# Attention weights turned unnormalized, with the reciprocal sums applied to the logits and the token rows

## The chip, the core and the metric

The kernel runs on one core of a Trainium2 chip. The metric is the time of one execution in device microseconds (us). The core has a matrix engine (PE, with its weight loads shown apart as PEld), a vector engine (DVE), a scalar engine (ACT) and a general engine (POOL), each working through its own instructions in order; a queue processor (SP) and POOL also issue transfers to and from memory.

## What is computed

Causal attention over a window of 128 positions, with a linear bias, for 8 batches of 576 tokens and 8 heads of 64, and behind it a mixture of 8 experts. A token picks its expert afresh or keeps that of the token before it, by the sign of a gate. Both the choice and the gate use linear maps of the attention's output.

```
scores = q @ k.T / 8 - slope[h] * |i - j|      where 0 <= i - j < 128, else -1e9
attn   = exp(scores - max);  attn = attn / (sum(attn) + 1e-9)
x      = (attn @ v), heads side by side        # [8, 576, 512]
logits = x @ w_gate;  local = sigmoid(x @ w_local)
e      = argmax(logits) if s == 0 or local < 0.5 else e of token s - 1
out    = softmax(logits)[e] * (relu(x @ w1[e]) @ w2[e])
```

The division by the sum is a factor per token and head. It can be applied to the weights, or later to the 64 columns of x that belong to the head.

## The kernel before, in words

**Attention.** The work is cut into 32 slots, one for a pair of heads of one batch (4 slots a batch), and a slot into 9 blocks of 64 queries. The function `spread` reads the list `ORDER[p]`, a table written out by hand, and emits one piece of work for each of its letters; since each engine works in program order, this table sets the order on all of them. A letter without a mark is work of the slot itself, one mark (`'`) means the slot before, two marks the one before that. Per slot the pieces are:

- `S` products of q and k on PE into tiles `sc` (four PSUM buffers); `D` bias, mask and row maximum on DVE (`scs`, `mn`); `E` the exponential on ACT, which also writes the row sums `sm`; its result lies in one of two buffers `PB`, shown in the trace as the tile `cut`.
- `R` adds 1e-9 to the sums and takes the reciprocal `r` on DVE, in three groups; `N` multiplies each of the 9 blocks of weights by its reciprocals on POOL, in place.
- `U` turns weights on PE (tile `pt`), `C` copies them out (`pts`, on DVE for `C0`, else on ACT), `M` multiplies them with v on PE (`xa`), `X` copies the result to `xT` on ACT, `T` transposes it on DVE into a buffer `T`. After the last `T` of a batch SP writes this buffer to memory (`xd`), as rows of tokens.

A dot in the table advances a side program by one step: `tokens(b)` (logits from `xT`, on PE, ACT and DVE) and `route(b)` (the expert of each token, its place in a table, and five scatters of entries to the table `t4` on POOL, the rows `t<-pay,to`). It begins with `X1` of the last pair of a batch, two slots late. Colons advance `setup`, which makes constants on POOL and also blanks `t4` in memory. In the last two batches POOL also gathers token rows of the first experts (`kr<-xd`, `wraw<-xd`), and ACT and DVE split the first weights.

**Experts.** Each weight chunk is cut into a high and a low part (ACT and DVE), and PE does three products for each pair of parts (lines 878 to 880, tiles `h` and `y`). The first two experts get only tokens of the first batches, so they can start before the last batch is routed; the third needs all of it: `tokens(7)` and `route(7)` then run as a side program of the first two (`routing`), one step with each `tick`, then come the table, the gathers on POOL and the turning of the rows on DVE.

Of the kernel before, what the change touches and what calls it, by code (L numbers as in the profile page):

```python
# [8 lines left out]
F32 = mybir.dt.float32  # L9
# [7 lines left out]
P = 128  # L17
# [33 lines left out]
def windows(nb):  # L51
# [6 lines left out]
ORDER = [  # L58
# [4 lines left out]
]  # L63
# [8 lines left out]
def moe_attention(ctx, tc, qT, kT_d, vv, wg, wl, w1, w2, out):  # L72
# [24 lines left out]
    msel = cp.tile([P, 4], F32, name="msel")  # L97
    roff = cp.tile([P, 1], F32, name="roff")
    first = cp.tile([P, NT], F32, name="first")
    w32 = cp.tile([P, 4, 32], F32, name="w32")  # L100
# [224 lines left out]
    with ExitStack() as actx:  # L325
# [11 lines left out]
        for s in range(3):  # L337
            V.append([ap.tile([P, n, P], F32, name=f"v{n}{z}{s}") for n, z in ((4, 0), (4, 1), (5, 2))])
        for s in range(2):
# [39 lines left out]

        loaded = load(0)  # L380

        warm = ap.tile([P, P], F16, name="warm")
        T = [ap.tile([P, SB, 4, 32], F32, name=f"T{s}") for s in range(2)]
        dve.memset(warm, 0.0)
        pw = ptk.tile([P, 512], F32, name="pk")
# [13 lines left out]
        for h in range(2):  # L399
            for z in range(2):  # L400
                dve.memset(slope[halves[h], z:z + 1], -4.0 if h == z else -2.0)
        for p in range(4):
            make_bias(p)
# [6 lines left out]
        def setup():  # L410

            whole = dict(channel_multiplier=0, allow_small_or_imprecise_dtypes=True)
            pool.memset(w32, 0.0)
            nc.sync.dma_start(w32[:, :, 0:8], wg.rearrange("(k p) e -> p k e", p=P))
            nc.sync.dma_start(w32[:, :, 8:9], wl.rearrange("(k p) e -> p k e", p=P))
            yield
# [31 lines left out]
            yield  # L448
            blank = spare.rearrange("p f (n w) -> p (f n) w", w=4)
            pool.memset(blank, 0.0)  # L450
            yield
            pool.memset(blank[:, :, 1], NOWHERE)
            rows = t4.rearrange("(p n) w -> p n w", p=P)
            nc.sync.dma_start(rows[:, 0:256], blank)
            nc.sync.dma_start(rows[:, 256:320], blank[:, 0:64])
            yield
            pool.memset(part[:, S:], 0.0)
# [9 lines left out]

        GROUPS = {3: slice(0, 4), 5: slice(4, 6), 8: slice(6, 9)}

        class Scores:  # L470


            def __init__(self, b, p, qb, k):
                self.p, self.qb, self.k, self.pbs = p, qb, k, PB[(4 * b + p) % 2]
                self.mn = sp.tile([P, 9], F32, name="mn")
                self.sm = sp.tile([P, 9], F32, name="sm")
                self.r = sp.tile([P, 9], F32, name="r")
                self.ps, self.sc = {}, {}
# [24 lines left out]

            def R(self, i):
                g = GROUPS[i]
                dve.tensor_scalar(self.r[:, g], self.sm[:, g], 1e-9, None, ALU.add)
                dve.reciprocal(self.r[:, g], self.r[:, g])

            def N(self, i):
                for j in range(GROUPS[i].start, GROUPS[i].stop):  # L510
                    pool.tensor_scalar(self.part(j), self.part(j), self.r[:, j:j + 1], 1.0, ALU.mult, ALU.mult)

        class Weigh:


            def __init__(self, b, p, v, xT):
                self.b, self.p, self.v, self.xT, self.pbs = b, p, v, xT, PB[(4 * b + p) % 2]
                self.pt, self.pts = {}, {}
# [53 lines left out]

            def T(self, j):
                if j == 0:
                    dve.transpose(T[self.b % 2][:, 0:12, self.p], self.xT[:, self.p, 0:384].rearrange("p (b i) -> p b i", i=32))
                else:
                    dve.transpose(T[self.b % 2][:, 12:SB, self.p], self.xT[:, self.p, 384:576].rearrange("p (b i) -> p b i", i=32))
# [4 lines left out]
        logits_of = {}  # L582

        def tokens(b, xT):

            L = tp.tile([P, NT, 9], F32, name="L")
            logits_of[b] = L
            for lo, n in ((0, 512), (512, 64)):
# [6 lines left out]
            read.append(b)  # L595
            for t0, n in ((0, 4), (4, 1)):
# [5 lines left out]
                yield  # L602

        def route(b):
# [64 lines left out]
            cn = tp.tile([P, NE], F32, name="cn")  # L669
            dve.tensor_scalar(ki, ri, 5, None, ALU.arith_shift_right)  # L670
            dve.tensor_scalar(ri, ri, 31, None, ALU.bitwise_and)
            dve.scalar_tensor_tensor(to, ri, float(NBLK), ki, ALU.mult, ALU.add)
# [62 lines left out]

        spare = wr.tile([P, 2, DM], F32, name="wraw")
        known, bumped, taken, routed, read, emitted = [], [], [], [], [], []
# [5 lines left out]
        def spread(order):  # L743
            for i, atom in enumerate(order.split()):
                yield atom
                if slot < LATE:
                    yield from {"N8": "::::::"}.get(atom.strip("'"), "")
                else:
                    if i % 11 == 0:
                        yield from ";,"  # L750
                    yield from {"N8": ":", "N3": ":"}.get(atom.strip("'"), "")

        for slot in range(4 * NB + DEPTH):
            b, p = divmod(slot, 4)
            if b < NB:
                if p == 0:
                    xT = tp.tile([P, 4, S], F32, name="xT")
                    qb, k = loaded
                    if slot == LATE:
                        run(chain(*prep.values()))  # L760
                        prep = {":": gathers(), ";": chain(*(early(e) for e in range(len(EARLY)))), ",": turns()}
                    if b == NB - 1:
                        W.load()
                pairs[slot] = Scores(b, p, qb, k), Weigh(b, p, V[slot % 3], xT)
            for atom in spread(ORDER[p]):
                if atom == ".":
                    next(side, None)
                    continue
                if atom in prep:
                    next(prep[atom], None)  # L770
                    continue
                kind, j, n = atom[0], int(atom[1]), slot - len(atom) + 2
                scoring = kind in "SDERN"
                if not 0 <= n < 4 * NB:
                    continue
                getattr(pairs[n][0 if scoring else 1], kind)(j)
                emitted.append((atom[:2], n))
                if emitted[-1] == ("S3", 0):
                    warmth(2)
                if kind == "X" and j == 1 and n % 4 == 3 and n < 4 * NB - 1:  # L780
                    run(side)
                    side = chain(tokens(n // 4, pairs[n][1].xT), route(n // 4))
            if 1 <= slot < 4 * NB - 1:
# [239 lines left out]
    def routing():  # L1023
        yield from chain(tokens(NB - 1, last_xT), route(NB - 1))
        e = len(OWN) - 1
# [132 lines left out]
```

## Time and profile before

| | us |
|---|---|
| median of 3 runs | 727.41 (726.89 to 727.48) |
| profiled execution | 728.06 |
| its span | 726.3 |
| busy in the span: PE, DVE, ACT, POOL | 684.9, 474.3, 418.8, 375.8 |

The span is that of the instructions; 1.76 us of the execution lie around it. Busy time is that in which the engine works on something; PE's instructions overlap, so a busy PE can still be slow, and the granted clock says how fast it was allowed to run (1.00 is 2.4 GHz, 0.50 is 1.2 GHz, a value between is a mean over the stretch).

### The profile page before, as it was taken

The numbers are of one execution on the slowest core, as the hardware profiler recorded it, in microseconds if no ns is written. First come the engines' busy times: TensorE is split into PE (matmuls) and PEld (weight loads), VectorE is DVE, ScalarE is ACT, GpSimd is POOL, SyncE is SP. The second block draws the span as 40 slices with busy tenths as digits, with TensorE's granted clock in tenths as the row PEclk, the third lists the DMA queues.
The fourth block names the chain that finished last, engine by engine and source line by source line (L and its number), as shares of the span: only waits on it lengthen the run. The fifth ranks groups of instructions, "written<-read, shape, count | busy, mean of one in ns | idle before, by whom it ended". The sixth has DMA issues, their size and how long they took to land.

```text
span 726.3 us, 17972 instructions
## 1 busy us (share of the span) xinstructions
PE 684.9 (94%) x6019; PEld 568.9 (78%) x6019; DVE 474.3 (65%) x1611; ACT 418.8 (58%) x1200; POOL 375.8 (52%) x594
## 2 busy tenths in 40 slices
PE   7897999999988699989999999999999999999996
PEld 4675767777766477968888889989989978888895
DVE  7576788788887769874463465477477467445562
ACT  5686888888878555353343454365365355334552
POOL 5755575675778763677743164453544545201321
PEclk9898999999999889999999999999999999999998
DMA  8797866766555366556544465566657547425550
GB/s 239 225 281 223 241 205 191 224 196 186 180 160 148 95 198 218 160 147 197 184 134 136 133 202 186 181 185 224 186 172 246 167 157 234 161 90 181 165 170 31
DMA packets 95217, 131.51 MB, mean 181 GB/s; under 512 B 12881, under 2 KB 66769, under 8 KB 95122
## 3 DMA queue, kind: packets, MB, share of 16 engines
q1 hardware_dynamic: 85234, 109.47, 49.3%
q0 software_dynamic: 9456, 20.27, 9.1%
q8 instruction: 48, 0.79, 0.5%
q10 hardware_dynamic: 432, 0.59, 0.3%
q14 instruction: 47, 0.39, 0.2%
HBM read 109.97 MB, written 20.91 MB: 180 GB/s over the span
## 4 chain that ended last, share of the span: by engine, by line
PE 73%; DVE 10%; issue 7%; POOL 4%; DMA 4%; ACT 1%; SPq 1%; POOLq 0%; DVEq 0%; ACTq 0%
PE y L880 9%; PE y L878 8%; PE y L879 8%; PE h L879 8%; PE h L880 8%; PE h L878 8%; PE xa L152 8%; PE sc L152 6%; PE pt L152 5%; PE pk L152 3%; POOL cut L152 2%; DVE scs L152 2%; DMA out<-y,sidx 1%; DVE cut L256 1%; POOL kr L167 1%
## 5 line engine op out<-in xcount | busy, mean ns | idle before, releaser
L256 DVE TENSOR_TENSOR cut<-wraw,cut 128x512 fp32r<-128x512 f32 x231 | 149.8, 687 | 53.6 <-ACT cut L254 52.3
L167 POOL DMA_INDIRECT kr<-xd,xidx x141 | 150.7, 1069 | 46.3 <-issue 39.3
L254 ACT CAST cut<-wraw 128x512 fp32r<-128x512 f32 x212 | 120.7, 618 | 55.0 <-PE y L880 54.7
L152 POOL TENSOR_SCALAR cut<-cut,r 128x192 f32<-128x192 f32 (+2 forms) x288 | 113.1, 411 | 68.9 <-ACT pts L152 23.1
L872 POOL DMA_INDIRECT out<-y,sidx x41 | 44.4, 1084 | 199.6 <-ACT y L887 165.2
L878 PE MATMUL h<-qx,cut 128*128 128x384 f32 (+6 forms) x440 | 141.3, 321 | 2.5 <-ACT qx L176 2.5
L879 PE MATMUL h<-qx,cut 128*128 128x384 f32 (+6 forms) x440 | 141.6, 322 | 0.4 <-DVE qx L177 0.4
L880 PE MATMUL h<-qx,cut 128*128 128x384 f32 (+6 forms) x440 | 141.6, 322 | 0.0
L152 ACT ACTIVATE cut<-scs,mn 128x192 f32<-128x192 f32 (+2 forms) x288 | 123.5, 432 | 22.3 <-DVE mn L152 20.5
L878 PE MATMUL y<-cut,hh 128*128 128x512 f32 x328 | 128.8, 393 | 2.0 <-ACT hh L923 1.1
L880 PE MATMUL y<-cut,hl 128*128 128x512 f32 x328 | 129.3, 395 | 1.1 <-DVE hl L924 1.0
L879 PE MATMUL y<-cut,hh 128*128 128x512 f32 x328 | 129.0, 393 | 0.0
L923 ACT ACTIVATE hh<-h 128x384 fp32r<-128x384 f32 (+6 forms) x103 | 47.4, 460 | 123.0 <-PE h L880 123.0
L924 DVE SCALAR_TENSOR_TENSOR hl<-h,hh 128x384 fp32r<-128x384 f32 (+6 forms) x112 | 56.7, 506 | 87.8 <-ACT hh L923 86.5
L152 DVE CUSTOM_DVE_ANT_0 scs<-sc,bias 128x192 f32<-128x192 f32 (+2 forms) x288 | 83.9, 321 | 23.6 <-PE sc L152 21.4
L878 PEld LDWEIGHTS h<-qx,cut 128*128 128x128 f32 x440 | 83.4, 190 | 9.5 <-ACT qx L176 2.9
L879 PEld LDWEIGHTS h<-qx,cut 128*128 128x128 f32 x440 | 83.4, 190 | 7.3 <-DVE qx L177 0.8
L152 PEld LDWEIGHTS xa<-pts,v 128*64 128x64 f32 x1664 | 69.8, 143 | 22.8 <-issue 10.3
L880 PEld LDWEIGHTS h<-qx,cut 128*128 128x128 f32 x440 | 83.5, 190 | 3.1
L152 PE MATMUL xa<-pts,v 128*64 128x64 f32 (+1 forms) x1664 | 83.5, 247 | 0.0
L152 PE MATMUL pt<-ident,cut 128*128 128x128 f32 x384 | 63.0, 293 | 19.3 <-POOL cut L152 19.0
L152 PE MATMUL sc<-kr,qx 64*64 64x192 f32 (+2 forms) x1280 | 76.1, 317 | 4.5 <-DVE mn L152 4.4
(173 smaller groups left out, 891.7 us busy)
## 6 DMA issues: line engine op xcount, KB each, us to landing
wraw<-w SPq DMA_DIRECT2D x120, 512.0 KB
xd<-T SPq DMA_DIRECT2D x8, 1152.0 KB
kr<-kT SPq DMA_DIRECT2D x31, 288.0 KB
qx<-qT SPq DMA_DIRECT2D x30, 288.0 KB
v<-v SPq DMA_DIRECT2D x32, 256.0 KB
v<-v SPq DMA_DIRECT2D x64, 128.0 KB
kr<-xd,xidx POOLq DMA_INDIRECT x141, 4.1
v<-v SPq DMA_DIRECT2D x32, 32.0 KB
```

The costliest lines, as they stand in the source:

```text
L152: ins = getattr(self.engine, name)(*args, **kw)
L167: queued(nc.gpsimd.indirect_dma_start(out=r, out_offset=None, in_=src[0:n, :], in_offset=bass.IndirectOffsetOnAxis(ap=col, axis=0), bounds ...
L254: scalar.copy(c[:, 0, f], raw[:, f])
L256: (pool if 2 * n + f == POOL_CUT else vector).tensor_tensor(c[:, 1, f], raw[:, f], c[:, 0, f], ALU.subtract)
L872: queued(nc.gpsimd.indirect_dma_start(out=out[:, :], out_offset=bass.IndirectOffsetOnAxis(ap=col, axis=0), in_=y, in_offset=None, bounds_c ...
L878: nc.tensor.matmul(o, ah, bh, start=start, stop=False)
L879: nc.tensor.matmul(o, ah, bl, start=False, stop=False)
L880: nc.tensor.matmul(o, al, bh, start=False, stop=stop)
L923: now.act.activation(hh, hp, AF.Relu)
L924: nc.vector.scalar_tensor_tensor(hl, hp, 0.0, hh, ALU.max, ALU.subtract)
```

## The change

The pieces `R` and `N` go. The weights are turned and multiplied with v as the exponential leaves them. Row sums of a batch are kept together (`SM`). At the start of `tokens(b)`, DVE adds 1e-9 and takes the reciprocals of all four pairs at once (`rb`), eight small products on PE bring them into two layouts (with the selector `rsel` and with `ident`), and ACT copies them out (`rn`). The logits are formed from unnormalized rows, separately for each half of a pair, and multiplied by the reciprocals on DVE before they are summed (`lw`). The token rows in `T` are multiplied on POOL, one pair at a time, by a new side program `scaled`, which advances along with the first one once the logit products of the batch are read; the write to `xd` follows its fourth step. The last batch's `T` takes a buffer of the keys. The table is blanked at the start, from zeros that DVE writes. Two shifts in `route` take their constant from a tile, and one third of v's tiles moves to another pool. `ORDER` is new; two marks remain the deepest.

```diff
 ORDER = [
-    "S0 C1'' U3'' . C2'' D0 U0' E6' E7' C3'' D1 C0' M1'' E8' N5' E0 M2'' X0'' . R8' E1 S2 S4 D2 D3 N8' D4 T0'' U1' . M3'' E2 E3 M4'' X1'' S6 D5 R3 D6 S8 D7 D8 E4 N3 U2' E5 R5 T1'' M0'",
...
+    ". E6' S0 S2 C0' M3'' E7' M4'' E8' . U1' U2' D0 . D1 . E0 D2 X1'' S4 C1' D3 D4 E1 S6 . M0' C2' M1' M2' S8 E2 . D5 T0'' E3 D6 E4 U3' X0' E5 T1'' D7 C3' U0 D8",
...
+        dve.memset(spare, 0.0)
+        dve.memset(blank[:, :, 1], NOWHERE)
+        rows = t4.rearrange("(p n) w -> p n w", p=P)
+        nc.sync.dma_start(rows[:, 0:256], blank)
+        nc.sync.dma_start(rows[:, 256:320], blank[:, 0:64])
...
-            def R(self, i):
-                g = GROUPS[i]
-                dve.tensor_scalar(self.r[:, g], self.sm[:, g], 1e-9, None, ALU.add)
-                dve.reciprocal(self.r[:, g], self.r[:, g])
-
-            def N(self, i):
-                for j in range(GROUPS[i].start, GROUPS[i].stop):
-                    pool.tensor_scalar(self.part(j), self.part(j), self.r[:, j:j + 1], 1.0, ALU.mult, ALU.mult)
...
-                    if self.p == 3:
-                        nc.sync.dma_start(xd[self.b * XR:self.b * XR + XR].rearrange("(b q) c -> q b c", q=P),
-                                          T[self.b % 2].rearrange("p b k j -> p b (k j)"))
...
+            dve.tensor_tensor(rb[:, :, 0:9], SM[b % 2], tiny, ALU.add)
+            dve.reciprocal(rb[:, :, 0:9], rb[:, :, 0:9])
+            yield
+            pk = ptk.tile([P, 512], F32, name="pk")
+            rows = pk[:, 0:72].rearrange("p (k i z) -> p k i z", k=4, z=2)
+            for z in range(2):
+                for o in range(2):
+                    pe.matmul(rows[:, :, o::2, z], rsel[:, z, o], rb[:, :, o:9:2], start=True, stop=True, skip_group_check=True)
...
+            act.copy(rn, pk[:, 0:112])
...
-                dve.tensor_reduce(L[:, t0:t0 + n], pk[:, :, :, 0:9].rearrange("p t k e -> p t e k"), AX.X, ALU.add)
-                yield
+                w = tp.tile([P, 16, 2, 9], F32, name="lw", bufs=1)[:, :4 * n]
+                dve.tensor_tensor(w, pk.rearrange("p t k (h f) -> p (t k) h f", h=2)[:, :, :, 0:9],
+                                  by_head[:, 4 * t0:4 * t0 + 4 * n].unsqueeze(3).broadcast_to([P, 4 * n, 2, 9]), ALU.mult)
+                dve.tensor_reduce(L[:, t0:t0 + n], w.rearrange("p (t k) h e -> p t e (k h)", k=4), AX.X, ALU.add)
+                yield
+
+        def scaled(b):
+
+            for p in range(4):
+                t = T[b][:, :, p]
+                pool.tensor_tensor(t, t, RN[b % 2][:, 18 * p:18 * p + 18].unsqueeze(2).broadcast_to([P, SB, 32]), ALU.mult)
+                if p == 3:
+                    nc.sync.dma_start(xd[b * XR:b * XR + XR].rearrange("(b q) c -> q b c", q=P), T[b].rearrange("p b k j -> p b (k j)"))
+                yield
+
+        def both(main, other, ready):
+
+            done = False
+            for _ in main:
+                if not done and ready():
+                    done = next(other, 1) is not None
+                yield
+            run(other)
```

Two places in the order of instructions show what moves. The first is POOL while one of the middle batches is routed; `cut<-cut,r` are the multiplications `N`, `t_76<-pay,to` the five scatters. Before:

```order
L678 DMA t_76<-pay,to 40960x4 x2
L152 TENSOR_SCALAR cut<-cut,r 128x192 x2
L678 DMA t_76<-pay,to 40960x4
L152 TENSOR_SCALAR cut<-cut,r 128x192 x3
L678 DMA t_76<-pay,to 40960x4
L152 TENSOR_SCALAR cut<-cut,r 128x64
L152 TENSOR_SCALAR cut<-cut,r 128x128
L152 TENSOR_SCALAR cut<-cut,r 128x192 x2
L678 DMA t_76<-pay,to 40960x4
L152 TENSOR_SCALAR cut<-cut,r 128x192 x5
```

The same engine after the change, from the last constant of the setup on; `T_161<-T_161,rn_95` is the multiplication of the token rows, one instruction for each pair:

```order
L160 IOTA io_83 128x32
L160 TENSOR_TENSOR T_161<-T_161,rn_95 128x18x32 x4
L731 DMA t_76<-pay,to 40960x4 x5
L160 TENSOR_TENSOR T_162<-T_162,rn_96 128x18x32 x4
L731 DMA t_76<-pay,to 40960x4 x5
```

Nothing that PE reads in attention stands on POOL any more, and nothing stands between the scatters. The second place is PE at the start of the experts; `h` and `y` are expert products, `pk<-xT,w_90` the logit products of the last batch. Before:

```order
L879 MATMUL h<-qx,xT 128x256
L152 MATMUL xa<-pts,v_126 64x64 x2
L152 MATMUL xa<-pts,v_125 64x128 x2
L152 MATMUL xa<-pts,v_127 64x64 x2
L152 MATMUL pk<-xT,w_90 32x512 x4
L880 MATMUL h<-qx,xT 128x256
```

And after, with `rb_94` the reciprocals of the last batch:

```order
L933 MATMUL h<-qx,xT 128x256
L931 MATMUL y<-cut,hh 128x512
L932 MATMUL y<-cut,hh 128x512
L931 MATMUL y<-cut,hh 128x512
L932 MATMUL y<-cut,hh 128x512
L933 MATMUL y<-cut,hl 128x512 x2
L160 MATMUL pk<-rb_94,rsel 128x4x5
L160 MATMUL pk<-rb_94,rsel 128x4x4
L160 MATMUL pk<-rb_94,rsel 128x4x5
L160 MATMUL pk<-rb_94,rsel 128x4x4
L160 MATMUL pk<-rb_94,ident 64x4x5 x4
```

The last batch's side program begins 24 `h` products and 6 `y` products into the experts, where it began 12 `h` products in, among the rest of attention; and it begins with the reciprocals.

## Rows read from the trace of the kernel before

**Rows 1.** The page: busy time, share of the span and instructions of each engine.
```profile
PE 684.9 (94%) x6019; PEld 568.9 (78%) x6019; DVE 474.3 (65%) x1611; ACT 418.8 (58%) x1200; POOL 375.8 (52%) x594
```

**Rows 2.** Chain of waits, first and last marker: start, duration, engine, tile, line.
```profile
44.48 1.46 PE pk L152 x8
...
260.66 1.46 PE pk L152 x8
```

**Rows 3.** Busy time between markers: length, five engines, granted clock, DMA share, GB/s.
```profile
9.56:44.48 34.92, 32.38 (x486) 25.06 (x489) 24.26 (x144) 28.22 (x117) 22.02 (x88) 0.86 0.79 226
44.48:78.65 34.17, 29.89 (x456) 22.52 (x459) 23.10 (x134) 25.08 (x97) 19.10 (x41) 0.90 0.87 261
78.65:107.06 28.41, 27.40 (x456) 20.64 (x459) 23.79 (x134) 24.65 (x97) 19.15 (x42) 1.00 0.71 213
192.69:223.73 31.04, 27.65 (x454) 20.82 (x455) 24.38 (x142) 24.75 (x99) 22.64 (x43) 1.00 0.46 131
223.73:260.66 36.93, 28.67 (x384) 21.78 (x387) 25.45 (x112) 22.46 (x77) 29.87 (x47) 0.86 0.39 110
260.66:326.90 66.24, 61.03 (x342) 50.91 (x341) 55.94 (x154) 35.29 (x72) 38.38 (x37) 1.00 0.63 195
326.90:726.30 399.40, 390.67 (x2070) 343.47 (x2070) 221.35 (x375) 182.73 (x351) 161.97 (x150) 0.99 0.54 169
```

**Rows 4.** Waits of PE up to 260 us: total us, times, longest.
```profile
PE pt L152 <- POOL cut L152: 19.0, 15, 4.2
...
PE pk L152 <- DVE OH L152: 2.0, 7, 0.3
```

**Rows 5.** Busy time in three stretches of low clock, columns as in Rows 3.
```profile
20.00:30.00 10.00, 9.94 (x127) 7.81 (x127) 4.64 (x27) 4.75 (x19) 5.88 (x23) 0.68 0.73 243
65.00:75.00 10.00, 6.57 (x76) 5.12 (x78) 3.73 (x23) 4.82 (x20) 8.93 (x15) 0.66 0.51 149
245.00:260.00 15.00, 9.39 (x82) 7.53 (x82) 6.07 (x13) 5.09 (x13) 12.47 (x15) 0.66 0.32 93
```

**Rows 6.** Timeline, POOL and PE at 65 us, POOL and DVE at 246 us.
```profile
65.10 1.20 POOL L678 DMA_INDIRECT t<-pay,to  x1 [3.40 <-DVE mn L152]
...
67.55 0.83 POOL L152 TENSOR_SCALAR cut<-cut,r 128x192 f32<-128x192 f32 x2
...
68.44 0.90 PE L152 MATMUL pt<-ident,cut 128*128 128x128 f32 x3 [3.90 <-POOL cut L152]
...
246.84 1.21 POOL L152 TENSOR_SCALAR cut<-cut,r 128x192 f32<-128x192 f32 x1
...
246.27 0.96 DVE L152 TENSOR_TENSOR xT<-wraw,xT 128x512 fp32r<-128x512 f32 x1
```

**Rows 7.** Groups of instructions that go: busy, mean ns, idle before, releasers.
```profile
L152 POOL TENSOR_SCALAR cut<-cut,r 128x192 f32<-128x192 f32 (+2 forms) x288 | 113.1, 411 | 68.9 <-ACT pts L152 23.1
...
L152 DVE TENSOR_SCALAR r<-sm 128x4 f32<-128x4 f32 (+2 forms) x96 | 20.0, 208 | 4.5 <-ACT cut L152 4.2
L152 DVE RECIPROCAL r<-r 128x4 f32<-128x4 f32 (+2 forms) x96 | 16.7, 174 | 3.3
```

**Rows 8.** Groups nearest in kind to what is added.
```profile
L152 POOL TENSOR_TENSOR cut<-wraw,cut 128x512 fp32r<-128x512 f32 x1 | 1.3, 1307 | 11.5 <-ACT cut L152 11.5
...
L152 PE MATMUL pk<-ident,part 128*128 128x128 f32 x40 | 7.5, 285 | 0.8 <-DVE L L152 0.8
L152 PE MATMUL pk<-onesb,hr 1*128 1x8 f16 x40 | 2.2, 164 | 0.0
```

**Rows 9.** Chain of waits from 263 us, then PE's waits from 260 to 330 us.
```profile
263.15 0.12 PE h L878
263.86 0.23 PE y L878
...
326.91 0.80 PE h L879
...
PE h L878 <- ACT qx L176: 2.5, 1, 2.5
```

More of the change, by code (lines that the diff above doesn't have):

```diff
@@ L98, in moe_attention @@
     roff = cp.tile([P, 1], F32, name="roff")
+    tiny = cp.tile([P, 4, 9], F32, name="tiny")
+    rsel = cp.tile([P, 2, 2, P], F32, name="rsel")
+    SM = [cp.tile([P, 4, 9], F32, name=f"sm{s}") for s in range(2)]
+    RB = [cp.tile([P, 4, 10], F32, name=f"rb{s}") for s in range(2)]
+    RN = [cp.tile([P, 112], F32, name=f"rn{s}") for s in range(2)]
+    LG = [cp.tile([P, NT, 9], F32, name=f"lg{s}") for s in range(2)]
+    c5 = cp.tile([P, NT], I32, name="c5")
+    c31 = cp.tile([P, NT], I32, name="c31")
     first = cp.tile([P, NT], F32, name="first")
@@ L337, in moe_attention @@
         for s in range(3):
-            V.append([ap.tile([P, n, P], F32, name=f"v{n}{z}{s}") for n, z in ((4, 0), (4, 1), (5, 2))])
+            v = (ap.tile([P, 13 * P], F32, name=f"v{s}") if s < 2 else vp.tile([P, 4 * DM], F32, name="cut")).rearrange("k (j c) -> k j c", c=P)
+            V.append([v[:, 0:4], v[:, 4:8], v[:, 8:13]])
         for s in range(2):
@@ L380, in moe_attention @@
         loaded = load(0)
+        spare = wr.tile([P, 2, DM], F32, name="wraw")
+        blank = spare.rearrange("p f (n w) -> p (f n) w", w=4)
         warm = ap.tile([P, P], F16, name="warm")
         T = [ap.tile([P, SB, 4, 32], F32, name=f"T{s}") for s in range(2)]
+        T = {b: T[b % 2] for b in range(NB - 1)}
         dve.memset(warm, 0.0)
@@ L413, in setup @@
             pool.memset(w32, 0.0)
-            nc.sync.dma_start(w32[:, :, 0:8], wg.rearrange("(k p) e -> p k e", p=P))
-            nc.sync.dma_start(w32[:, :, 8:9], wl.rearrange("(k p) e -> p k e", p=P))
+            wgk, wlk = (w.rearrange("(k p) e -> p k e", p=P) for w in (wg, wl))
+            for h in range(2):
+                nc.sync.dma_start(w32[halves[h], :, 16 * h:16 * h + 8], wgk[halves[h]])
+                nc.sync.dma_start(w32[halves[h], :, 16 * h + 8:16 * h + 9], wlk[halves[h]])
+            yield
+            for z in range(2):
+                for o in range(2):
+                    for g in range(2):
+                        c = 64 * (g ^ o) + 32 * z
+                        pool.tensor_copy(rsel[:, z, o, 64 * g:64 * g + 64].rearrange("p (a c) -> p a c", a=2),
+                                         ident[:, c:c + 32].unsqueeze(1).broadcast_to([P, 2, 32]))
+                yield
+            for x in RB:
+                pool.memset(x, 1.0)
+            for x in LG:
+                pool.memset(x, 0.0)
             yield
@@ L574, in T, with batch_side @@
                 if j == 0:
-                    dve.transpose(T[self.b % 2][:, 0:12, self.p], self.xT[:, self.p, 0:384].rearrange("p (b i) -> p b i", i=32))
+                    dve.transpose(T[self.b][:, 0:12, self.p], self.xT[:, self.p, 0:384].rearrange("p (b i) -> p b i", i=32))
                 else:
-                    dve.transpose(T[self.b % 2][:, 12:SB, self.p], self.xT[:, self.p, 384:576].rearrange("p (b i) -> p b i", i=32))
-                    if self.p == 3:
-                        nc.sync.dma_start(xd[self.b * XR:self.b * XR + XR].rearrange("(b q) c -> q b c", q=P),
-                                          T[self.b % 2].rearrange("p b k j -> p b (k j)"))
+                    dve.transpose(T[self.b][:, 12:SB, self.p], self.xT[:, self.p, 384:576].rearrange("p (b i) -> p b i", i=32))
         logits_of = {}
+        def batch_side(b, xT):
+            return both(chain(tokens(b, xT), route(b)), scaled(b), lambda: b in read and ("T1", 4 * b + 3) in emitted)
         def tokens(b, xT):
-            L = tp.tile([P, NT, 9], F32, name="L")
+            L, rb, rn = LG[b % 2], RB[b % 2], RN[b % 2]
             logits_of[b] = L
+            dve.tensor_tensor(rb[:, :, 0:9], SM[b % 2], tiny, ALU.add)
[3 more added lines that the diff above has]
+            rows = pk[:, 0:72].rearrange("p (k i z) -> p k i z", k=4, z=2)
+            for z in range(2):
+                for o in range(2):
+                    pe.matmul(rows[:, :, o::2, z], rsel[:, z, o], rb[:, :, o:9:2], start=True, stop=True, skip_group_check=True)
+            for h in range(2):
+                for o in range(2):
+                    g = h ^ o
+                    pe.matmul(pk[halves[o], 72 + 20 * h:92 + 20 * h].rearrange("p (t k) -> p k t", k=4), ident[:, 64 * g:64 * g + 64],
+                              rb[:, :, o::2], start=True, stop=True, skip_group_check=True)
+            yield
+            act.copy(rn, pk[:, 0:112])
+            yield
             for lo, n in ((0, 512), (512, 64)):
@@ L746, in spread @@
                 if slot < LATE:
-                    yield from {"N8": "::::::"}.get(atom.strip("'"), "")
+                    yield from {"E8": "::::::"}.get(atom.strip("'"), "")
                 else:
@@ L750, in spread @@
                         yield from ";,"
-                    yield from {"N8": ":", "N3": ":"}.get(atom.strip("'"), "")
+                    yield from {"E8": ":", "E3": ":"}.get(atom.strip("'"), "")
         for slot in range(4 * NB + DEPTH):
@@ L772, in moe_attention @@
                 kind, j, n = atom[0], int(atom[1]), slot - len(atom) + 2
-                scoring = kind in "SDERN"
+                scoring = kind in "SDE"
                 if not 0 <= n < 4 * NB:
@@ L781, in moe_attention @@
                     run(side)
-                    side = chain(tokens(n // 4, pairs[n][1].xT), route(n // 4))
+                    side = batch_side(n // 4, pairs[n][1].xT)
             if 1 <= slot < 4 * NB - 1:
@@ L1023, in routing @@
     def routing():
-        yield from chain(tokens(NB - 1, last_xT), route(NB - 1))
+        yield from batch_side(NB - 1, last_xT)
         e = len(OWN) - 1
```

27 lines of the change are left out of this document (12 added, 15 removed), and 6 rows, old and new, of the table ORDER.

## The prediction, made before the changed kernel ran

> **What bounds the kernel now.** The page comes first: PE is busy for 94% of the span [rows 1]. That does not make PE the bound everywhere, since its busy time holds waits inside overlapping products, so the next view is the chain of waits, and in it a marker that returns once per batch: the first logit product. The first stands at 44.48 us and the last at 260.66 [rows 2]; the eight markers and 326.9, where the third expert begins, cut the run into stretches. Their busy times [rows 3] show three kinds. From 78.65 to 163.91 there are three batches of 28.41 to 28.43 us (the first is shown) with PE busy 27.40 at full clock: there PE is the bound, with 1.0 us to gain at most. The first two stretches and the last two of attention are longer than their PE work: the batch from 44.48 takes 34.17, the one from 192.69 takes 31.04, the last 36.93, although its PE busy time is about that of the others. Behind 326.9 PE is busy for 390.67 of 399.40 us, and the change does not touch it.
>
> What ends PE's idle time up to 260 us is mostly one thing: turning (`pt`) waits for POOL's multiplied weights (`cut`), 15 times, 19.0 us [rows 4]. A place at 65 us shows how [rows 6]: POOL issues a scatter late, after 3.40 us of waiting, two multiplications stand behind it, and PE waits 3.90 us for them. In the last batch POOL is busy 29.87 of 36.93 us [rows 3], with gathers and scatters between the multiplications. What an idle PE costs beyond the wait is seen in the granted clock [rows 5]: 0.68 from 20 to 30 us, and 0.66 in the two other stretches, which is a mean of 1.2 and 2.4 GHz; the second of them follows the 3.90 us of waiting just named.
>
> **The change, part by part.**
>
> *Multiplications `N` and reciprocals `R`.* POOL loses 288 instructions, 113.1 us; DVE loses 192, 20.0 + 16.7 = 36.7 us [rows 7], 4.6 a batch. Neither time counts by itself. What counts is that turning now waits for ACT's exponential alone: the 19.0 us of waits on POOL go. With them goes the slow clock behind them: in the stretches of [rows 5] PE was busy 9.94, 6.57 and 9.39 us at a clock that was 0.32, 0.34 and 0.34 short of full, which is 3.2 + 2.2 + 3.2 = 8.6 us of work at full clock. Together 27.6 us. The bounds: nothing of it, if another engine is just behind POOL; and some 29, if the 1.0 us a batch of the middle ones goes too.
>
> *Products on PE.* Eight small products per batch are new, with 128-column weights and up to 20 columns moved. Two groups lie on both sides: `pk<-onesb,hr` at 2.2 us over 40, 0.055 each, and the turning of the logits at 7.5 over 40, 0.19 each [rows 8]. So 0.44 to 1.5 us a batch; I take 0.7, nearer to the short ones, since the moved columns are few, and PE has nothing to hide it in: 8 x 0.7 = 5.6 us (3.5 to 12).
>
> *A longer side chain.* Reciprocals on DVE, products, a copy on ACT, and only then the logit products, all in one PSUM buffer. PE waits in program order, and behind it score products queue up. The wait of this kind that exists, for `OH`, is 2.0 us over 7, 0.3 each [rows 4]. I take one such per batch, 8 x 0.3 = 2.4 us (0 to 5).
>
> *Scaling the token rows.* 32 instructions on POOL of 576 elements; the one POOL tensor product shown takes 1.307 us for 512 [rows 8], so 1.47 each, 5.9 a batch, where POOL gives up 113.1 / 8 = 14.1. Nothing in PE's attention waits for it; the write to `xd`, which waits, feeds gathers of later stages. Cost nothing, hidden by POOL's idle time of about 9 us in a batch [rows 3] plus the 8 that it gains; without that cover, 47 us. One row bears on what POOL and DVE do to each other: at 246.84 one multiplication took 1.21 us against a mean of 0.411 [rows 7], while DVE's subtraction, which reads two tiles, ran from 246.27 for 0.96 us [rows 6]. So they do hold each other up, by up to 0.8 us. The Trainium skill has the rule on its page "SBUF — State Buffer", section "SBUF: two separate sides": VectorE and GpSimd share one pair of ports, and whichever starts first keeps it for its whole instruction, so that the other stands still. The trace agrees in that one place. By the rule alone each scaling could hold up DVE for its whole 1.47 us; it is the slower rival below.
>
> *DVE and ACT.* The new work of DVE per batch (two operations for all sums, two products and two wider reductions) is six operations: at the 0.2 us of [rows 7] 1.2 us, and 3 if the wider ones take thrice that, against 4.6 that go. ACT gets one short copy. ACT is busy 24.65 of 28.41 us, DVE 23.79 [rows 3]: DVE gets free time, ACT stays as it is, 3.5 us behind PE. Cost nothing. The zeros for the table (1,280 elements a partition) lie in DVE's start, where it waits for POOL's masks anyway; at POOL's 1307 ns for 512 elements [rows 8] they would be 3.3 us, and that is the upper bound of what they delay. The earlier blanking puts 640 KB ahead of the second batch's loads; at the 226 GB/s of that stretch [rows 3] 2.9 us of transfer, for data of which the first is used a slot or two later. Nothing either.
>
> *The hand-over to the experts.* The last batch's side program now begins 24 `h` and 6 `y` products into the experts, not 12 `h` products. At 0.12 and 0.23 us [rows 9] that is 24 x 0.12 + 6 x 0.23 - 12 x 0.12 = 2.8 us later, and its reciprocals add about 1 us. The third expert already waits for this chain before it starts at 326.91: 2.5 us for its rows, still turned on ACT [rows 9]. So a later chain moves it by as much. Part of that is won back, since the chain no longer competes with multiplications; I take 3.0 us (0 to 8).
>
> **The sum.** 728.06 - 27.6 + 5.6 + 2.4 + 3.0 = 711.5 for the profiled execution, which is 0.65 above the median: 710.8, say 711 us. A second way gives nearly the same: the stretches of [rows 3] beyond the 28.4 of a middle batch are 5.8, 2.6 and 8.5, and of the first, with PE busy 32.38 at 0.86, some 4.5 of 34.92: 21.4; middle batches stay, since 0.7 + 0.3 of new work takes the place of the 1.0 idle; less 3.0, it is 18.4, or 709.0 against the median.
>
> **The rivals.**
>
> *Another engine right behind POOL.* In the first stretch ACT is busy 28.22 of 34.92 us, in middle batches 24.65 of 28.41 [rows 3]; turning now waits on ACT's exponential, and in the first batches the DMA share is 0.79 and 0.87, so loads may come late once PE is faster. Half of the 27.6 us stays: 711 + 13.8 = 725. Against it: of PE's waits POOL's 19.0 is by far the longest line, the one shown beside it 2.0 [rows 4].
>
> *The third expert eats more.* If its rows come 8 us later, not 3, and no work is left to fill the time: 716. For it speaks that two tables, a gather in 16 steps and the turning of the rows stand one behind the other before it; against it, that POOL is busy only 38.38 of 66.24 us there [rows 3].
>
> *More than forecast.* The new table runs without any of the small waits: middle batches at 27.4 + 0.7, the hand-over free of charge: 711 - 3 x 0.3 - 2.4 - 3.0 and a cheaper set of products (-2) = 703.
>
> *Slower: scalings that hold up DVE.* If each of the 32 scalings stops DVE and this reaches PE, through bias and maximum (`D`) to the four score buffers, 32 x 1.47 = 47 us come on top: 758. The kernel becomes slower once more than 16.4 / 32 = 0.51 us of each gets through. For it: the row at 246.84. Against it: POOL's multiplications took 2.4 times that time in the same place, and DVE has 8 us to spare in a batch after the change, against 5.9 of scalings.
>
> **How the numbers follow.** The forecast has a chance of 0.55, with a range of its own of 705 to 717. Another engine behind POOL 0.17, the third expert 0.12, more than forecast 0.10, slower 0.06. The range of 8 in 10 leaves out the slower case, half of the first rival and some of the fast one: 701 to 723. What measurement can tell from no change is 0.2%, 1.5 us. Faster by more: all but the slow case and a little of the first rival, 0.91; within it 0.03; slower 0.06.
>
> **What would show it.** Right: PE's waits on POOL are gone from the attention part, the granted clock stays at 1.00 from 30 us to the hand-over, the marker of the last batch (now the first product of `rb`) stands near 240 us and the middle batches take 28.0 to 28.7. The eight products take about 0.7 us a batch; the third expert begins some 64 to 70 us after that marker. Wrong would be: middle batches above 29 us with PE waiting for ACT or DVE, a low clock in a new place, loads that PE waits for between 30 and 80 us, or the third expert more than 75 us after the marker.

## The result and the profile after

The changed kernel takes 718.5 us (median of 4 runs, 716.8 to 719.7), the kernel before 727.4 in the same series: a ratio of 0.9877, with a 95% interval of 0.9856 to 0.9898. The forecast was 711 us with a range of 701 to 723; the gain is 8.9 us where 16.4 were forecast. The profiled execution took 718.23 us, 9.8 less than the one before (span 716.5 against 726.3).

The page of the changed kernel, busy time and share of the span, answers to [rows 1]:

```profile
PE 684.4 (96%) x6147; PEld 574.3 (80%) x6147; DVE 457.4 (64%) x1456; ACT 416.3 (58%) x1208; POOL 300.2 (42%) x348
```

PE's waits up to 322 us, in total, times and longest, answer to [rows 4]:

```profile
PE h L931 <- ACT qx L184: 4.8, 1, 4.8
PE sc L160 <- DMA v<-v: 4.4, 1, 4.4
PE y L933 <- DVE hl L977: 4.3, 2, 3.5
PE y L931 <- ACT hh L160: 2.9, 3, 1.8
PE pk L160 <- DVE OH L160: 2.0, 7, 0.3
...
PE pk L160 <- DVE rcb L160: 0.9, 2, 0.8
```

The line of 19.0 us for POOL's `cut` has gone, and none of its size has come in attention. The 4.4 us for a load of v end at 9.59 us; the kernel before stood at the same place until 9.56 us, there for DVE, so this wait costs nothing new, and the zeros and the early blanking of the table cost nothing either. What has come or grown stands behind attention: 3.5 us for `hl`, and 4.8 us for the third expert's rows, where it was 2.5. PE's new products, start and duration, and after them the stretches of the run (columns as in [rows 3]; the markers are now the first `rb` products):

```profile
69.80 1.07 PE L160 MATMUL pk<-rb,rsel 128*128 128x20 f32 x8
70.80 0.42 PE L160 MATMUL pk<-rb,ident 128*64 128x20 f32 x8
71.14 0.88 PE L160 MATMUL pt<-ident,cut 128*128 128x128 f32 x6
```

```profile
69.80:98.02 28.22, 27.70 (x473) 21.58 (x469) 20.70 (x113) 24.43 (x99) 9.38 (x9) 1.00 0.94 254
...
183.11:211.68 28.57, 28.00 (x475) 21.69 (x471) 21.69 (x122) 24.41 (x99) 13.58 (x13) 1.00 0.54 140
211.68:241.36 29.68, 26.42 (x382) 20.67 (x379) 23.78 (x96) 23.74 (x81) 16.68 (x15) 1.00 0.52 141
241.36:315.77 74.41, 63.52 (x338) 53.19 (x336) 58.02 (x150) 32.80 (x67) 48.22 (x45) 0.90 0.57 173
315.77:716.50 400.73, 392.50 (x2072) 344.59 (x2072) 222.14 (x376) 182.85 (x351) 163.31 (x151) 0.99 0.54 169
...
15.00:240.00 225.00, 218.33 (x3660) 170.50 (x3658) 165.34 (x876) 195.01 (x769) 76.22 (x72) 1.00 0.78 211
245.00:265.00 20.00, 15.70 (x87) 12.65 (x84) 16.61 (x26) 8.10 (x17) 13.20 (x12) 0.79 0.61 176
...
315.00:321.00 6.00, 5.23 (x12) 3.84 (x13) 0.75 (x2) 0.62 (x1) 4.66 (x5) 0.50 0.97 320
```

From 15 to 240 us the granted clock is 1.00, where [rows 5] had 0.66 to 0.68 in three places. (From 10 to 15 us, behind the wait for v, it is 0.56.) Attention is all that was promised; the loss lies between 241 and 321 us. The account, made at the first logit product: it starts at 243.16 us (at 260.66 before, [rows 2]), 17.5 us earlier, and by then PE has done 15 `h` and 6 `y` products of the experts more than before, at the prices of [rows 9] another 3.2 us. So attention gained 20.7 us. The third expert's first product stands at 315.77 us. In the kernel before it stands at 325.78; the 326.9 of [rows 3] and [rows 9], which the prediction takes for it, is its second:

```profile
325.78 0.73 PE L878 MATMUL h<-qx,cut 128*128 128x512 f32 x2 [2.48 <-ACT qx L176]
```

From the first logit product to there it takes 315.77 - 243.16 = 72.6 us against 325.78 - 260.66 = 65.1, with those 3.2 us of work already done: 10.7 us lost. Behind it 0.2 us more are lost (400.73 against 726.30 - 325.78 = 400.52). 20.7 - 10.7 - 0.2 = 9.8.

Where the 10.7 us begin is seen in the timeline, first POOL, DVE and PE of the changed kernel (start, duration, engine, line, operation):

```profile
247.94 1.17 POOL L160 TENSOR_TENSOR kr<-kr,rn 128x576 f32<-128x576 f32 x1
...
250.59 1.17 POOL L160 TENSOR_TENSOR kr<-kr,rn 128x576 f32<-128x576 f32 x1
...
253.26 1.17 POOL L160 TENSOR_TENSOR kr<-kr,rn 128x576 f32<-128x576 f32 x1
...
255.91 1.18 POOL L160 TENSOR_TENSOR kr<-kr,rn 128x576 f32<-128x576 f32 x1
...
246.29 3.97 DVE L264 TENSOR_TENSOR cut<-wraw,cut 128x512 fp32r<-128x512 f32 x4 [2.52 <-ACT cut L160]
...
250.52 0.44 DVE L160 TENSOR_TENSOR lw<-pk,rn 128x288 f32<-128x288 f32 x1
250.89 1.44 DVE L264 TENSOR_TENSOR cut<-wraw,cut 128x512 fp32r<-128x512 f32 x1
252.25 0.68 DVE L160 TENSOR_REDUCE lg<-lw 128x36 f32<-128x288 f32 x1
252.84 4.80 DVE L264 TENSOR_TENSOR cut<-wraw,cut 128x512 fp32r<-128x512 f32 x3
...
258.18 0.80 PE L933 MATMUL y<-cut,hl 128*128 128x512 f32 x1 [3.55 <-DVE hl L977]
```

The last batch's four scalings (its rows lie in a `kr` buffer) run here beside the subtractions that split the experts' weights (`cut`). The subtraction begun at 250.89 ends at 252.33, 0.57 us after the scaling of 250.59 has ended, as if it had begun only then. `hl` stands behind three of them, and PE waits 3.55 us for it; behind that, the clock is low (0.66 from 255 to 265 us).

### The profile page after: what moved, and what is told of

It reads as the page before. It is cut to its first block, busy times and chain, and to the rows that moved or that the text cites. A ratio compares the mean times of both kernels' runs of the same rounds, so it can differ in the third digit from the quotient of the medians.

```text
span 716.5 us, 17525 instructions
## 1 busy us (share of the span) xinstructions
PE 684.4 (96%) x6147; PEld 574.3 (80%) x6147; DVE 457.4 (64%) x1456; ACT 416.3 (58%) x1208; POOL 300.2 (42%) x348
## 5 line engine op out<-in xcount | busy, mean ns | idle before, releaser
L264 DVE TENSOR_TENSOR cut<-wraw,cut 128x512 fp32r<-128x512 f32 x231 | 155.6, 712 | 56.1 <-ACT cut L262 50.5
L175 POOL DMA_INDIRECT kr<-xd,xidx x141 | 152.6, 1082 | 42.9 <-issue 39.3
L931 PE MATMUL h<-qx,cut 128*128 128x384 f32 (+6 forms) x440 | 143.1, 325 | 4.8 <-ACT qx L184 4.8
L933 PE MATMUL h<-qx,cut 128*128 128x384 f32 (+6 forms) x440 | 143.1, 325 | 0.0
L932 PE MATMUL h<-qx,cut 128*128 128x384 f32 (+6 forms) x440 | 143.0, 325 | 0.0
L931 PEld LDWEIGHTS h<-qx,cut 128*128 128x128 f32 x440 | 84.7, 192 | 13.8 <-ACT qx L184 5.2
L932 PEld LDWEIGHTS h<-qx,cut 128*128 128x128 f32 x440 | 84.7, 192 | 7.2 <-DVE qx L185 0.4
L933 PEld LDWEIGHTS h<-qx,cut 128*128 128x128 f32 x440 | 84.6, 192 | 3.3 <-issue 0.2
L731 POOL DMA_INDIRECT t<-pay,to x40 | 40.5, 1014 | 96.9 <-DVE cn L160 73.3
L160 PE MATMUL sc<-kr,qx 64*64 64x192 f32 (+2 forms) x1280 | 73.8, 312 | 5.7 <-DMA v<-v 4.4
L933 PEld LDWEIGHTS y<-cut,hl 128*128 128x128 f32 x328 | 61.9, 189 | 20.2 <-DVE hl L977 7.3
L931 PEld LDWEIGHTS y<-cut,hh 128*128 128x128 f32 x328 | 62.2, 190 | 15.2 <-ACT hh L160 3.6
L932 PEld LDWEIGHTS y<-cut,hh 128*128 128x128 f32 x328 | 62.2, 190 | 10.5
```

What stands on the lines that cost most here:

```text
L160: ins = getattr(self.engine, name)(*args, **kw)
L175: queued(nc.gpsimd.indirect_dma_start(out=r, out_offset=None, in_=src[0:n, :], in_offset=bass.IndirectOffsetOnAxis(ap=col, axis=0), bounds ...
L264: (pool if 2 * n + f == POOL_CUT else vector).tensor_tensor(c[:, 1, f], raw[:, f], c[:, 0, f], ALU.subtract)
L731: ins = nc.gpsimd.indirect_dma_start(out=t4[:, :], out_offset=bass.IndirectOffsetOnAxis(ap=to[0:n, t:t + 1], axis=0), in_=pay[0:n, b, t], ...
L931: nc.tensor.matmul(o, ah, bh, start=start, stop=False)
L932: nc.tensor.matmul(o, ah, bl, start=False, stop=False)
```

## The experiments

Three theories were put to the test. **Theory 1**: the last batch's scalings hold up DVE's subtractions, and PE behind them. **Theory 2**: the last batch's write to `xd`, which now waits for the scalings, holds up the weight loads that stand behind it on SP. **Theory 3**, the prediction's own term: the routing chain of the last batch begins later in the experts' work and has three more steps.

| kernel | median us | ratio to before, 95% |
|---|---|---|
| changed kernel | 718.5 | 0.9877 (0.9856 to 0.9898) |
| `no_scale7b` | 711.9 | 0.9807 (0.9787 to 0.9827) |
| `no_scale` | 711.8 | 0.9794 (0.9777 to 0.9811) |
| `write7_pool_b` | 720.0 | 0.9912 (0.9892 to 0.9932) |
| `scale7_dve` | 714.1 | 0.9826 (0.9802 to 0.9850) |
| `double7` | 720.0 | 0.9919 (0.9896 to 0.9943) |
| `early7b` | 712.0 | 0.9810 (0.9786 to 0.9834) |
| `spaced7` | 712.1 | 0.9810 (0.9788 to 0.9831) |
| `later7` | 711.1 | 0.9807 (0.9782 to 0.9832) |

**Four runs that settle nothing.** The first series ran on a chip on which the kernel before itself took 767.1 us (761 to 774 in 11 runs): `no_scale7` 806.5, `write7_pool` 802.9, `early7` 786.2, `head7` 790.0 us. The times that were expected cannot be read from them. On that chip all four kernels with the change are slower than the kernel before, by 2.7 to 4.8%, and leaving out the last batch's scalings (806.5) is no faster than keeping them with the write moved (802.9). The changed kernel itself was not measured there, so what follows holds for the other chips. Three of the four kernels were run once more on those. `head7` was not; what the early reciprocals alone are worth stays open.

> Leaves out the four scalings of the last batch (its rows reach the experts unscaled); the write to xd then waits for the transposes alone. The changed kernel takes 718.5 us, and PE waits 3.6 us for hl at 258. If the scalings hold up DVE through a shared port (theory 1), that wait goes with the slow clock behind it: 711 to 713. If the late write to xd holds the weight loads behind it on SP (theory 2), the same gain comes, with DVE's subtractions unchanged at 1.6 us apiece in that place. If what costs is that the routing chain begins late and has three more steps (theory 3), at most 1 us: 718.

> The write of the last batch's rows to xd is issued from POOL's queue, not SP's, so that no weight load stands behind it. Theory 2: the loads go out some 6 us earlier and 3 to 6 us return, 713 to 715. Theories 1 and 3: 718, with the 3.6 us wait for hl still there.

> The last batch's reciprocals, eight products and copy are issued in attention's last slots, as soon as its sums stand, and each of its four scalings as soon as its rows are transposed; both are then done before the experts' work begins. All three theories expect a gain: the scalings meet no subtraction of the experts, the write to xd stands ahead of the loads, the chain is three steps shorter. 718.5 less 6 (theory 1) less 2 (three steps) = 710 if PE's tail of attention is not disturbed; 716 if it is.

> Only the reciprocals, products and copy of the last batch are issued early, the scalings stay where they are, beside the experts. Theory 3: the three steps are some 2 us of work between ticks, the third expert begins 2 to 4 us earlier: 714.5 to 716.5. Theories 1 and 2: the 3.6 us wait for hl remains, within 1 us of 718.5.

**Without the last batch's scalings.** In `scaled`:

```diff
-                pool.tensor_tensor(t, t, RN[b % 2][:, 18 * p:18 * p + 18]...
+                if b < NB - 1:
+                    pool.tensor_tensor(t, t, RN[b % 2][:, 18 * p:18 * p + 18]...
```

> Leaves out the last batch's four scalings (its rows reach the experts unscaled), once more. Theory 1: 711 to 713, PE's wait of 3.6 us for hl at 258 gone, DVE's subtractions there back at 0.7 us. Theory 3: 717 to 719, since the chain of the last batch is as long and as late as before.

It took 711.9 us. DVE, PE and a stretch of this kernel, to be held against the changed kernel's:

```profile
245.19 2.50 DVE L264 TENSOR_TENSOR cut<-wraw,cut 128x512 fp32r<-128x512 f32 x4 [1.64 <-ACT cut L160]
...
248.30 0.68 DVE L264 TENSOR_TENSOR cut<-wraw,cut 128x512 fp32r<-128x512 f32 x1
248.90 0.70 DVE L160 TENSOR_REDUCE lg<-lw 128x36 f32<-128x288 f32 x1
249.52 1.89 DVE L264 TENSOR_TENSOR cut<-wraw,cut 128x512 fp32r<-128x512 f32 x3
...
308.52 0.75 PE L932 MATMUL h<-qx,cut 128*128 128x512 f32 x1 [4.40 <-ACT qx L184]
...
245.00:265.00 20.00, 17.16 (x122) 14.47 (x114) 18.24 (x46) 10.88 (x26) 10.78 (x9) 1.00 0.81 263
```

The same eight subtractions take 2.50 + 0.68 + 1.89 = 5.1 us, not 3.97 + 1.44 + 4.80 = 10.2: 5.1 us less, for four scalings of 1.17. PE does 17.16 us of work at full clock from 245 to 265 us, where it did 15.70 at 0.79, which is 12.4: 4.8 us more. Some 0.7 us of this is not the scalings' doing: in the changed kernel the clock is 0.75 from 245 us to the first scaling at 247.94 already, and it is 1.00 there in `write7_pool_b` below, which is held up alike. From the `rb` marker (241.13) the third expert begins after 67.4 us instead of 74.4. By the medians the four scalings cost 6.6 us, by the ratios 0.7% or 5.1.

PE's wait for `hl` is not yet the price. The third expert waits for its rows in both kernels (4.8 and 4.40 us), so what sets its start is the routing chain of the last batch, whose steps on DVE stand behind the held subtractions. POOL's first scatter of that batch shows it, in the kernel before, the changed kernel and this one:

```profile
284.16 1.03 POOL L678 DMA_INDIRECT t<-pay,to  x1 [2.29 <-DVE cn L152]
...
273.94 1.36 POOL L731 DMA_INDIRECT t<-pay,to  x1 [4.55 <-DVE cn L160]
...
266.41 1.37 POOL L732 DMA_INDIRECT t<-pay,to  x1 [4.55 <-DVE cn L160]
```

From the batch's first logit product to this scatter it takes 284.16 - 260.66 = 23.5 us before, 273.94 - 243.16 = 30.8 in the changed kernel, and 266.41 - 242.92 = 23.5 without the four scalings. From the scatter to the third expert all three take 41.6 to 42.1 us. So the scalings lengthen the chain by 7.3 us, all of it ahead of the scatter. That they make POOL itself late, for the gathers and scatters behind them, is ruled out as the cause: POOL stands idle ahead of the scatter and waits for DVE.

**The write from another queue.**

```diff
-                    nc.sync.dma_start(xd[b * XR:b * XR + XR]...
+                    (nc.gpsimd if b == NB - 1 else nc.sync).dma_start(xd[b * XR:b * XR + XR]...
```

> The write of the last batch's rows is issued from POOL's queue, behind its scalings, so that on SP no weight load stands behind it; all else as in the changed kernel. Without the scalings 711.9 us were measured. Theory 2 (the gain came from loads that no longer wait behind the write): 712 to 714 here too. Theory 1 (port): 717 to 719, the wait of 3.6 us for hl stays.

720.0 us: no gain, so the loads behind the write were not what the scalings delayed. PE of this kernel waits as before:

```profile
256.24 0.79 PE L933 MATMUL y<-cut,hl 128*128 128x512 f32 x1 [3.80 <-DVE hl L977]
```

Theory 2 falls.

**The scalings on DVE.**

```diff
-                pool.tensor_tensor(t, t, RN[b % 2][:, 18 * p:18 * p + 18]...
+                (dve if b == NB - 1 else pool).tensor_tensor(t, t, RN[b % 2][:, 18 * p:18 * p + 18]...
```

> The last batch's four scalings are done on DVE, not on POOL; the write still waits for them, on SP. Theory 1: no stretched subtraction is left, but DVE has some 4 x 0.65 = 2.6 us more to do, 712 to 715. Theory 2: the write is as late as before, 717 to 719.

714.1 us, with five runs from 711.8 to 721.1; the profiled one is the slowest. Its subtractions (group of instructions from 240 to 265 us: count, busy, mean ns) are back at their own time, although the write is as late as before:

```profile
L264 DVE TENSOR_TENSOR cut<-wraw,cut 128x512 fp32r<-128x512 f32 x10 | 6.6, 693 | 2.3 <-ACT cut L160 2.3
```

In the changed kernel the same group has a mean of 1180 ns. The scalings take 0.75 us each on DVE, 3.0 in all, less than what they cost from POOL.

**Without any scaling.** The line of `scaled` is left out for all batches.

> Leaves out the scalings of all eight batches (all rows reach the experts unscaled). The rival that they hold up DVE in attention too: middle batches shorter than 28.3 us, and clearly under the 711.9 us of the run that leaves out the last batch's alone, by up to 28 x 1.2 us. If they are hidden in the middle batches, as the prediction had it: 711 to 713.

711.8 us, and the middle batches take 28.3 us with and without their scalings: the 28 scalings of the other batches cost nothing. Why those are free shows in the changed kernel itself, POOL and then DVE in the middle of attention:

```profile
99.87 4.50 POOL L160 TENSOR_TENSOR T<-T,rn 128x576 f32<-128x576 f32 x4 [4.74 <-ACT rn L160]
...
102.06 0.55 DVE L160 COPY pts<-pt 128x384 f32<-128x384 f32 x1
102.53 0.35 DVE L160 CUSTOM_DVE_ANT_0 scs<-sc,bias 128x192 f32<-128x192 f32 x1
...
102.80 0.57 DVE L160 STREAM_TRANSPOSE T<-xT 128x384 f32<-128x384 f32 x1
103.30 0.32 DVE L160 CUSTOM_DVE_ANT_0 scs<-sc,bias 128x192 f32<-128x192 f32 x1
```

Four scalings run in one piece, and DVE works beside them at its usual pace (0.32 us is the mean of the bias and maximum operation over attention). These operations read one tile from SBUF and one from PSUM, or one tile alone. So does `lw` at 250.52 in the changed kernel, which met a scaling and took 0.44 us; without scalings it takes 0.45. Of the operations looked at, only those with two inputs in SBUF were held.

**Twice the scalings.**

```diff
-                pool.tensor_tensor(t, t, RN[b % 2][:, 18 * p:18 * p + 18]...
+                for _ in range(2 if b == NB - 1 else 1):
+                    pool.tensor_tensor(t, t, RN[b % 2][:, 18 * p:18 * p + 18]...
```

> Each of the last batch's four scalings is done twice on POOL (the rows reach the experts scaled twice). Leaving the four out gave 711.9 us against 718.5, 1.7 us for each. Theory 1 (each scaling that runs beside the experts' subtractions holds DVE up for its time, and PE behind it): four more cost 4 x 1.2 to 4 x 1.7 us, 723 to 726, with PE's wait for hl longer than 3.6 us. If the price was that of one unlucky meeting, not of each scaling: 718 to 720.

720.0 us, 1.5 more than the changed kernel and hardly apart from it. The 723 to 726 that theory 1 gave here are missed: the price is not one of each scaling. DVE, POOL and PE of this kernel, and its first scatter:

```profile
257.11 0.18 DVE L160 TENSOR_REDUCE rm<-lg 128x5 f32<-128x40 f32 x1
...
257.89 1.47 DVE L160 TENSOR_TENSOR ra<-lg,rm 128x40 f32<-128x40 f32 x1
259.40 1.19 DVE L160 TENSOR_TENSOR ra<-ra,k 128x40 f32<-128x40 f32 x1
...
258.12 2.40 POOL L160 TENSOR_TENSOR kr<-kr,rn 128x576 f32<-128x576 f32 x2
...
261.08 0.38 PE L160 MATMUL pk<-identb,rcb 128*1 128x128 f16 x4 [2.44 <-DVE rcb L160]
...
275.08 1.36 POOL L732 DMA_INDIRECT t<-pay,to  x1 [6.51 <-DVE cn L160]
```

The pairs reach past the subtractions. There they meet `ra`, two tiny products of SBUF tiles with a mean of 200 ns, which take 1.47 and 1.19 us. The eight subtractions take 2.50 + 2.02 + 3.67 = 8.2 us here, less than the 10.2 with single scalings, since the first pair comes later. So the chain from the first logit product (244.00) to the scatter is 31.1 us, hardly more than the 30.8 of the changed kernel. What counts is how many operations of this kind stand in the scalings' way, and who waits for them.

**The scalings before the experts' work.** Three versions issue the last batch's reciprocals, products and copy in attention's last slots and each scaling once its rows are transposed. The core of the first, `early7b` (`tail` advances at the dots of the order, once the sums stand); `spaced7` and `later7` put more dots between the steps of `head`:

```diff
+        def ends():
+            yield from head(NB - 1)
+            s = scaled(NB - 1)
+            for p in range(4):
+                while ("T1", 4 * NB - 4 + p) not in emitted:
+                    yield
+                next(s, None)
+                yield
+            run(s)
```

> The last batch's reciprocals, products, copy and scalings before the experts' work, once more, on a chip whose runs of the kernel before stand near 727 us. Theory 1 (scalings hold up DVE beside the experts) and theory 3 (a chain that is late and three steps longer) both expect 708 to 713 us, with no wait for hl near 255 us; if instead the hand-over is bound by something that the last batch's scalings do not touch, 716 to 719.

> As in the run with the last batch's reciprocals, products, copy and scalings issued early (712.0 us), with twice the distance between the three steps, so that PE does not wait for the reciprocals (0.9 us) and for ACT's copy (0.6 us) near 233 us. If these two waits caused the granted clock of 0.83 between 235 and 262 us, the clock is 1.00 there and some 4 us return: 707 to 709. If not, 712.

> As the run with the last batch's scalings issued early (712.0 us), but the eight products stand 16 products later in PE's order, behind work that does not need the reciprocals. The waits of 0.9 and 0.6 us near 233 us should go, and with them the granted clock of 0.55 between 235 and 245 us, where PE was busy 9.9 us: up to 4.4 us return, 707.5 to 709. If the clock falls in any case when attention hands over, 712; if the later scalings meet the subtractions again, 713 to 716.

712.0, 712.1 and 711.1 us: some 7 us faster than the changed kernel, and no faster than leaving the four scalings out. The wait for the third expert's rows falls from 4.8 to 0.7 us in the first, yet this is paid for elsewhere. DVE and PE of the first, and its stretch from 235 us:

```profile
240.54 2.14 DVE L160 TENSOR_TENSOR xT<-wraw,xT 128x512 fp32r<-128x512 f32 x1
...
232.84 1.06 PE L160 MATMUL pk<-rb,rsel 128*128 128x20 f32 x8 [0.88 <-DVE rb L160]
...
235.08 2.40 PE L160 MATMUL xa<-pts,v 128*64 128x64 f32 x32 [0.63 <-ACT xT L160]
...
235.00:245.00 10.00, 9.92 (x70) 6.18 (x71) 7.02 (x8) 6.73 (x15) 8.52 (x8) 0.55 0.24 72
```

Behind two waits of 0.88 and 0.63 us PE is granted 0.55 of its clock from 235 to 245 us: 9.92 x 0.45 = 4.5 us. And the scalings still meet DVE: the split of two SBUF tiles at 240.54 takes 2.14 us, where it takes 0.69 alone. Twice the distance between the steps did not move the products in PE's order (the first of the two waits is still there, 0.9 us, and the clock is 0.56 with that one alone). In the third version they stand later, the two waits are gone and the clock is 1.00 there, but the scalings now meet six subtractions at once. POOL, DVE and PE of the third:

```profile
237.91 4.51 POOL L160 TENSOR_TENSOR kr<-kr,rn 128x576 f32<-128x576 f32 x4
...
237.93 8.07 DVE L160 TENSOR_TENSOR cut<-wraw,cut 128x512 fp32r<-128x512 f32 x6
...
243.04 0.50 PE L955 MATMUL y<-cut,hh 128*128 128x512 f32 x1 [2.27 <-DVE cut L160]
```

The six, which take 3.67 us in the changed kernel at 236.62, take 8.07: 4.4 us more, for 4.5 us of scalings, which themselves take no longer than the 4.50 us in the middle of attention. DVE stood still for nearly all of them. Behind PE's wait of 2.27 us the clock falls too, to 0.66 from 245 to 250 us. The 713 to 716 us that were expected for this case did not come, though: here the scalings hold DVE up ahead of the routing chain's logits, and the third expert waits only 1.4 us for its rows.

## Why the prediction was right in its direction and short of its size

**Right: the removal.** PE's 19.0 us of waits for POOL and the slow clock behind them are gone; at the first logit product of the last batch the terms 27.6 - 5.6 - 2.4 make 19.6 us, and the trace shows 20.7. That the sum meets so closely is in part luck, since two of these terms are off, as follows.

**Mis-sized, and evened out: the products.** They hold PE for 71.14 - 69.80 = 1.34 us a batch, not 0.7, 10.7 us and not 5.6, within the 3.5 to 12 given. The four with `rsel` take 1.00 of it, the four with `ident` 0.34. The middle batches stay at 28.2 to 28.6 us all the same. PE's idle time there took in half a microsecond of the products (0.5 us is left of 28.22, where 1.0 was), and the eight logit products give back about 0.4 (1.07 us at 71.95, where [rows 2] has 1.46); the rest was not traced.

**Nearly nothing: the longer side chain in attention.** 2.4 us were set down. The waits for `OH` are the 2.0 us of before; only `rcb` brings a new 0.9.

**The step that failed: "Cost nothing, hidden by POOL's idle time", for the scalings.** It asked whether POOL had time, and who waits for the rows. It did not ask what DVE does in the same microseconds. For 28 of the 32 scalings it holds (`no_scale`). The last four lie in the experts' work, where DVE subtracts one SBUF tile from another, and there they cost 5 to 7 us: they hold up DVE, and with it the routing chain that the third expert waits for, by 7.3 us. That is nearly the whole of the 718.2 - 711.5 = 6.7 us by which the sum missed the profiled execution: without these four the kernel takes 711.9, and 711 was forecast.

**The hand-over's own term** (3.0, with bounds of 0 to 8) was the place where this showed: 10.7 us by the account above. Without the four scalings the same account gives 308.52 - 242.92 + 3.2 - 65.1 = 3.7 us, close to the forecast: the term had the later chain about right and lacked what the scalings do to it. Behind the third expert's start another 1.1 us are lost in that run (401.58 against 400.52), for which the sum has no term and whose cause was not tested. The third expert's rows come last as forecast (a wait of 4.8 us, 2.5 before [rows 9]), with a clock of 0.50 for the 6 us behind it.

**The rivals.** The slower one had the right mechanism and the wrong place: it let scalings stop DVE's bias and maximum (`D`) in attention, which they leave alone, and priced 32 of them. The page "SBUF — State Buffer" of the Trainium skill says more than the prediction took from it, in a bracket of the section that it cites and in full in "Who interferes with whom": VectorE contends with a GpSimd instruction that reads SBUF when it has two SBUF inputs itself, and with at most one, outside modes that no run here tells apart, it does not. The trace agrees on each of these: `cut` and `ra` are held, `lw`, the bias and maximum, copy and transposes are not. With that condition the 32 scalings could have been sorted into 28 and 4 beforehand, from the inputs in the code and the order, a few tiny routing products aside. "The third expert eats more" came near in time (716) and had the place right: its rows come later, and PE waits for them. Its reason does not hold: tables, gathers and turning take as long as before, 41.8 us against 41.6 from the first scatter on, and the delay is there ahead of them. Another engine right behind POOL did not show: from 30 to 240 us no line of PE's waits is longer than the 2.0 us for `OH`.

**The checks named.** Of the marks given, four were hit: no waits on POOL in attention, the clock of 1.00 from 30 us on, the middle batches, and the last marker at 241.36 (240 forecast). The eight products miss theirs (1.34 for 0.7). The third expert begins 74.4 us after the last marker, where 64 to 70 was right and more than 75 wrong; without the four scalings it is 67.4. And one sign of being wrong came: a low clock in a new place, 0.79 from 245 to 265 us.

**Open.** How the change fares on the chip of the first series; whether early reciprocals alone shorten the hand-over (`head7`); and a version below 711 us, with the scalings neither beside two-tile operations of DVE nor bought with waits of PE at the end of attention.

## What to carry to other kernels

Before work goes to an idle POOL, list what DVE runs at that moment: here an operation with two inputs in SBUF was held by POOL's multiplications of SBUF tiles, one with an input from PSUM was not. Work that is free in 28 places can cost in the other 4, so price the last turn of a pipeline by itself, where other code runs beside it. And a wait of PE of less than a microsecond can have a second price, so look at the granted clock behind it: 0.55 behind the 0.88 and 0.63 us of `early7b`, yet 1.00 behind waits of 1.19 and 1.78 us in `no_scale7b`.

## What was not expected of the hardware

In `later7` POOL's scalings were not slowed by the six subtractions that stood still beside them: 4.51 us for four, 4.50 where nothing held them. It is not always so one-sided: pairs of scalings that met subtractions in `double7` took 2.75 us, and the pair that met `ra` 2.40. On one chip the kernel before took 767 us where it takes 727 on the others, and the kernels with the change 786 to 807 there; in the profile of `early7` PE stops 27 times before `xa`, 16.0 us in all, for nothing that the profile shows. The cause was not found.
